# Zero fill moved from chunk 1 into chunk 0 with its own place, and attention steps at other places of chunks 1 to 4

## The chip, the cores and the metric

One core of a Trainium2 chip runs the program alone. The metric is the device time of one execution in microseconds, given as the median of three runs. A profile shows one more execution, engine by engine: TensorE (PE, with its weight loads as PEld), VectorE (DVE), ScalarE (ACT), GpSimd (POOL) and the queue of SyncE (SP), which issues nearly all DMAs.

## What is computed

Three stages follow each other. Their inputs are float32, except `w_in` and `w_out`, which come as 64-bit floats.

```python
B, H, S, D = 4, 8, 576, 64                       # attention, two masks
scores = scale * q @ k.T                         # heads 0-3: the last 32 keys; heads 4-7: every 32nd key
x = softmax(masked scores) @ v                   # reshaped to 2304 tokens x 512
h = x @ w_in                                     # 512 -> 2048
x = (h * clip(h + 3, 0, 6) / 6) @ w_out          # 2048 -> 512
logits = x @ w_gate                              # 8 experts, the best one is taken
e = argmax(logits); g = softmax(logits)[e]; o = sigmoid(x @ w_output_gate)[e]
out = g * o * (relu(x @ w1[e]) @ w2[e])          # 512 -> 1024 -> 512
```

## The kernel before, in words

The 2304 tokens go through the dense layer in six chunks of 384 (c = 0 to 5). In each chunk a loop runs over 16 blocks f of 128 hidden units. `m1(c, f)` does 12 matmuls into a PSUM tile `h`; ACT and DVE make `r` of it (L534, L535) and then the two halves of `gh` (L540, L545); `m2(c, f - 1)`, nine matmuls of 512 columns, adds the block before into three accumulators. Each value is split in two float32r parts, so products take three matmuls.

Attention is cut into 32 groups. Group n passes through three steps: scores (L401, tiles `sa`, `sb`), then the softmax on DVE, ACT and POOL (L413, L418, L422 to L424), transposes (L451, tiles `ta`, `tb`), and the product with v (L468, tile `o`), which ACT and DVE write into `xh` and `xl`, the input of `m1`. One tick does scores of n, transposes of n - 1 and the product of n - 2. Eight ticks stand ahead of chunk 0, the others inside the chunks 0 to 4; the table `AT` says at which f of a chunk its ticks stand, and a chunk that has no entry spreads them evenly. A chunk can start only when the groups that write its tokens are through.

In chunk 0 the 64-bit weights are also loaded (SP, L182, tiles `rawi`, `rawo`, 512 KB each) and converted, on ACT (L192, L193, L216), DVE (L202 to L218) and POOL (L207, L218).

After each chunk the router picks the expert of each token (tile `rt`, allocated in pool `r_p` with one buffer of tag "rt") and POOL scatters the rows of the tokens into a DRAM table `xs_d` (L664). The table has to be zero at its first rows of each expert. `zero_fill` does this: a DVE instruction makes a tile of 132 zeros on each partition (out of `r`, with a bitwise and with 0), and eight DMAs of 792 KB each on SP's queue copy it to the regions of the eight experts. In the kernel before, the zero tile `z` is allocated in `r_p` under tag "rt" too, so the first router tile `rt0` has to wait until `z` has been read.

A scheduler orders the instructions on each engine at build time, the ticks of chunks 1 to 4 with raised priority; each engine then runs its list in order. SP's queue is in order too: an issue that waits for a buffer holds back those behind it.

`o_s` is a small tile that lives through the whole kernel; its only use is in chunk 5 and later, when the experts are put in order (`o_rest`, `o_over`).

Of the kernel before, what the change touches and what calls it, by code (L numbers as in the profile page):

```python
# [22 lines left out]
def kernel(  # L23
# [71 lines left out]
    acc = const.tile([128, NTILE + 1, E], F16, name="acc")  # L95
    cnt = const.tile([128, 8, E], F32, name="cnt")
    o_m = const.tile([128, 2], F32, name="o_m")
    o_s = const.tile([128, 2, E, E], F32, name="o_s")
    eid = const.tile([128, E], F32, name="eid")
    capc = const.tile([128, E], F32, name="capc")  # L100
    first_i = const.tile([128, 1], I32, name="first_i")
# [41 lines left out]
        nc.sync.dma_start(out=wgo[:, :, 0:E], in_=w_gate.rearrange("(c p) e -> p c e", p=128))  # L143
        nc.sync.dma_start(out=wgo[:, :, E:2 * E], in_=w_ogate.rearrange("(c p) e -> p c e", p=128))

    zf = []

    def zero_fill(es):
        if not zf:

            zf.append(r_p.tile([128, XW // 4], F32, tag="rt", name="z"))
            nc.vector.tensor_scalar(out=zf[0].bitcast(I32), in0=gh_t[1, 0][1][:, 0:XW // 4].bitcast(I32), scalar1=0,
                                    scalar2=None, op0=ALU.bitwise_and)
        z = zf[0]
        r = CAPS[0] // 128
        for e in es:
            nc.sync.dma_start(
                out=xs_d[e * NT:e * NT + r * 128, :].rearrange("(p r) (a c) -> p (r a) c", p=128, a=4),
                in_=z.unsqueeze(1).to_broadcast([128, r * 4, XW // 4]),
            )  # L160

# [533 lines left out]
    def o_rest():  # L697

        V = nc.vector
        ps = counts(NTILE, "cnt")  # L700
        V.tensor_copy(cnt[:, 0, :], ps)

        V.scalar_tensor_tensor(out=cnt[:, 2, :], in0=cnt[:, 0, :], scalar=float(E), in1=prio, op0=ALU.mult,
                               op1=ALU.add)
        V.scalar_tensor_tensor(out=cnt[:, 2, :], in0=cnt[:, 1, :], scalar=65536.0, in1=cnt[:, 2, :], op0=ALU.mult,
                               op1=ALU.add)
        sh = [128, E, E]
        key = cnt[:, 2, :]
        V.tensor_tensor(out=o_s[:, 0], in0=key.unsqueeze(1).to_broadcast(sh), in1=key.unsqueeze(2).to_broadcast(sh),
                        op=ALU.is_gt)  # L710
        V.tensor_reduce(out=cnt[:, 3, :], in_=o_s[:, 0], axis=AX.X, op=ALU.add)

        V.tensor_tensor(out=o_s[:, 0], in0=cnt[:, 3, :].unsqueeze(1).to_broadcast(sh),
                        in1=eid.unsqueeze(2).to_broadcast(sh), op=ALU.is_equal)
        V.tensor_tensor(out=o_s[:, 1], in0=o_s[:, 0], in1=eid.unsqueeze(1).to_broadcast(sh), op=ALU.mult)
        V.tensor_reduce(out=cnt[:, 4, :], in_=o_s[:, 1], axis=AX.X, op=ALU.add)
        V.tensor_copy(order_i, cnt[:, 4, :])

    def o_over():

        V = nc.vector
        sh = [128, E, E]
        V.tensor_tensor(out=o_s[:, 1].rearrange("p a e -> p e a"), in0=o_s[:, 0].rearrange("p a e -> p e a"),
                        in1=capc.unsqueeze(1).to_broadcast(sh), op=ALU.mult)
        V.tensor_reduce(out=cnt[:, 5, :], in_=o_s[:, 1].rearrange("p a e -> p e a"), axis=AX.X, op=ALU.add)

        V.tensor_scalar(out=cnt[:, 6, :], in0=cnt[:, 7, :], scalar1=float(RA), scalar2=None, op0=ALU.is_lt)
        V.tensor_tensor(out=cnt[:, 6, :], in0=cnt[:, 6, :], in1=cnt[:, 1, :], op=ALU.mult)
        V.tensor_tensor(out=cnt[:, 7, :], in0=cnt[:, 7, :], in1=cnt[:, 5, :], op=ALU.subtract)
        V.tensor_tensor(out=cnt[:, 7, :], in0=cnt[:, 7, :], in1=cnt[:, 6, :], op=ALU.mult)  # L730
        V.tensor_tensor(out=cnt[:, 5, :], in0=cnt[:, 5, :], in1=cnt[:, 7, :], op=ALU.add)
        V.tensor_tensor(out=cnt[:, 6, :], in0=cnt[:, 0, :], in1=cnt[:, 5, :], op=ALU.subtract)
# [222 lines left out]
    def convert():  # L955
# [3 lines left out]
        for stage, i in ((cv_3, n - 2), (cv_2, n - 1), (cv_1, n)):  # L959
            if 0 <= i < len(wq):  # L960
# [9 lines left out]
             2: [(t, N2, NG) for t in range(3, 10)],  # L970
             3: [(t, N2, NG) for t in range(10, 16)],
             4: [(t, N2, NG) for t in range(16, NG - N2 + 2)]}
    AT = {0: [0, 1, 2, 4, 5, 7, 9, 12]}
    for t in range(T0):
        with tc.high_priority(offset=0):
            at_tick(t, 0, 2 * GPB, alt=True)
# [11 lines left out]
    for c in range(NCH):  # L988
        steps = STEPS.get(c, [])
        at_f = AT.get(c, [i * KF // len(steps) for i in range(len(steps))])  # L990

        def step(f, parts):
            for f2, a in zip(at_f, steps):
                sub = "".join(x for x in (a[4] if len(a) > 3 else "pts") if x in parts)
                if f2 == f and sub:
                    with tc.high_priority(offset=150 if c else 0):
                        at_tick(*a[:3], False, sub)

        for f in range(KF):
            if c == 0:  # L1000
                loads(wl[1] + 4)
                for _ in range(CONVERTS[f]):
                    convert()
            m1(c, f)
            if f:
                for fn in todo[:1]:
                    fn()
                todo = todo[1:]
            step(f, "pt")
            if c == 1 and f < E // 2:  # L1010
                zero_fill([2 * f, 2 * f + 1])
# [242 lines left out]
```

## Time and profile before

| | |
|---|---|
| median of three runs | 879.62 us (879.28 to 881.7) |
| the profiled execution, its own time | 878.62 us |
| its span, first to last instruction | 876.8 us |
| PE / PEld / DVE / ACT / POOL busy | 93 / 83 / 55 / 46 / 19 % |

The span is what the views of the trace cover; the execution's own time is 1.8 us longer, and lies 1.0 us under the median. Runs of this kernel differ by some tenths of a per cent. Busy shares are averages over stages with different limits.

### The profile page before, as it was taken

The page shows a single profiled execution, that of the slowest core. Times are in us where ns is not written, and L with a number is a line of the kernel's source. Part 1 is how long each engine was busy: PE and PEld are TensorE (multiplying, and loading weights), DVE is VectorE, ACT ScalarE, POOL GpSimd, SP SyncE. Part 2 cuts the span into 40 slices and gives each one's busy share as a digit, 9 for nine tenths or more (in the row PEclk, how much of TensorE's full clock was granted, in tenths as well). Part 3 has the DMA queues.
Part 4 walks back from the last instruction along what each step waited for, and adds up shares of the span by engine and source line. Part 5 has one row for each costly group of instructions (what it writes and reads, how often), then busy time and mean ns, then how long its engine had stood idle before and what let it go on. Part 6 is the DMA issues. An engine that isn't in the chain of part 4 may idle for free. (4 is left out here: it accounts for less than half of the span.)

```text
span 876.8 us, 14855 instructions
## 1 busy us (share of the span) xinstructions
PE 815.7 (93%) x5040; PEld 726.2 (83%) x5041; DVE 485.4 (55%) x1394; ACT 405.3 (46%) x1055; POOL 166.0 (19%) x232
## 2 busy tenths in 40 slices
PE   6879888799499999989998999999999999999996
PEld 4668667678488888778887899998899999999995
DVE  4578998852253535534354332335656746766771
ACT  4577766743133533444344422324434545555551
POOL 3355554430021101111021010010011011011110
PEclk9558888999699999979997999999999999999999
DMA  4876222209922211322133000015158556566640
GB/s 132 247 215 184 78 77 93 82 28 201 163 70 41 38 22 28 89 49 46 28 73 74 1 21 18 1 62 158 48 147 235 168 168 185 170 183 210 199 133 20
DMA packets 179191, 91.71 MB, mean 105 GB/s; under 512 B 101369, under 2 KB 165113, under 8 KB 179112
## 3 DMA queue, kind: packets, MB, share of 16 engines
q1 hardware_dynamic: 175992, 81.15, 36.7%
q0 software_dynamic: 3120, 9.59, 2.9%
q8 instruction: 40, 0.66, 0.3%
q14 instruction: 39, 0.32, 0.1%
HBM read 74.63 MB, written 16.60 MB: 104 GB/s over the span
## 5 line engine op out<-in xcount | busy, mean ns | idle before, releaser
L530 PE MATMUL h<-xh,wi 128*128 128x384 f32 x768 | 228.7, 358 | 9.4 <-ACT xh L479 3.4
L554 PE MATMUL x<-wo,gh 128*128 128x512 f32 x864 | 230.6, 402 | 6.7 <-DVE gh L545 4.6
L554 PEld LDWEIGHTS x<-wo,gh 128*128 128x128 f32 x864 | 159.7, 190 | 37.4 <-DVE gh L545 7.0
L530 PEld LDWEIGHTS h<-xh,wi 128*128 128x128 f32 x768 | 148.2, 199 | 19.0 <-ACT xh L479 4.0
L530 PE MATMUL h<-xl,wi 128*128 128x384 f32 x384 | 136.7, 356 | 2.0 <-DVE xl L480 2.0
L535 DVE SCALAR_TENSOR_TENSOR r<-r,h 128x384 f32<-128x384 f32 x96 | 52.8, 550 | 117.1 <-ACT r L534 115.8
L424 POOL TENSOR_TENSOR p<-p,st 126x126 f32<-126x126 f32 (+4 forms) x80 | 56.6, 723 | 244.3 <-DVE st L423 151.9
L534 ACT ACTIVATE r<-h,three 128x384 f32<-128x384 f32 x96 | 55.5, 578 | 94.9 <-PE h L530 67.0
L418 ACT ACTIVATE p<-p,st 96x128 f32<-96x128 f32 (+2 forms) x176 | 67.2, 386 | 57.4 <-DVE st L413 57.3
L545 DVE TENSOR_TENSOR gh<-r,gh 128x384 fp32r<-128x384 f32 x96 | 60.0, 625 | 43.7 <-ACT gh L540 41.9
L540 ACT ACTIVATE gh<-r 128x384 fp32r<-128x384 f32 x96 | 50.3, 524 | 68.9 <-DVE r L535 63.5
L530 PEld LDWEIGHTS h<-xl,wi 128*128 128x128 f32 x384 | 76.6, 200 | 6.6 <-DVE xl L480 2.8
L851 ACT ACTIVATE hh<-eh 128x128 fp32r<-128x128 f32 (+7 forms) x64 | 26.3, 411 | 102.2 <-PE eh L844 94.9
L852 DVE SCALAR_TENSOR_TENSOR hh<-eh,hh 128x128 fp32r<-128x128 f32 (+7 forms) x64 | 29.3, 458 | 74.6 <-ACT hh L851 67.3
L891 POOL DMA_INDIRECT out_dram<-yo,e_i x21 | 21.3, 1015 | 190.9 <-ACT yo L927 186.8
L664 POOL DMA_INDIRECT xs_d<-x2r,idx x18 | 18.8, 1047 | 185.0 <-DVE idx L635 137.6
L401 PE MATMUL sb<-kT,qT 64*96 64x128 f32 (+2 forms) x176 | 35.9, 333 | 4.6 <-DVE st L413 2.2
L401 PEld LDWEIGHTS sb<-kT,qT 64*96 64x96 f32 (+2 forms) x176 | 25.6, 199 | 13.3 <-issue 5.5
L418 ACT ACTIVATION_READ_ACCUMULATOR p<-p,st 96x1 f32 (+2 forms) x176 | 33.5, 190 | 0.0
L468 PE MATMUL o<-pt,v 128*64 128x96 f32 (+2 forms) x352 | 31.1, 301 | 1.3 <-ACT pt L453 1.1
L401 PE MATMUL sa<-kT,qT 64*96 64x128 f32 (+2 forms) x176 | 32.2, 325 | 0.0
L451 PE MATMUL tb<-ident,p 96*128 96x96 f32 (+2 forms) x88 | 17.1, 300 | 15.2 <-DVE rt L599 11.8
(259 smaller groups left out, 1565.9 us busy)
## 6 DMA issues: line engine op xcount, KB each, us to landing
rawi<-in_moe_w_in_dram SPq DMA_DIRECT2D x16, 512.0 KB
rawo<-in_moe_w_out_dram SPq DMA_DIRECT2D x16, 512.0 KB
xs_d<-z SPq DMA_DIRECT2D x8, 792.0 KB
xs<-xs_d SPq DMA_DIRECT2D x28, 128.0 KB
qr<-in_q_dram SPq DMA_DIRECT2D x48, 72.0 KB
kr<-in_k_dram SPq DMA_DIRECT2D x48, 72.0 KB
v<-in_v_dram SPq DMA_DIRECT2D x20, 160.0 KB
er0i<-in_moe_w_dram SPq DMA_DIRECT2D x8, 256.0 KB
```

What stands on the lines that cost most here:

```text
L401: nc.tensor.matmul(s[h2][0:qn, j, 0:kn], lhsT=qt[p0:p0 + 64, q0:q0 + qn], rhs=kt[p0:p0 + 64, k0:k0 + kn], start=True, stop=True)
L418: nc.scalar.activation(out=p[h2][0:qn, j, 0:kn], in_=p[h2][0:qn, j, 0:kn], func=ACTF.Exp, bias=st[0:qn, h2, 0, j:j + 1], scale=-1.0, accum ...
L424: nc.gpsimd.tensor_tensor(out=p[h2][0:qn, j:j + c, 0:kn], in0=p[h2][0:qn, j:j + c, 0:kn], in1=st2.unsqueeze(2).to_broadcast([qn, c, kn]), ...
L468: nc.tensor.matmul(o[64 * h2:64 * h2 + 64, q0 - q00:q0 - q00 + qn], lhsT=vt[0:kn, i, :], rhs=pt[h2][0:kn, j, 0:qn], start=True, stop=True)
L530: nc.tensor.matmul(h, lhsT=w[:, a, kt, :], rhs=x[:, kt, c0:c0 + CH], start=(n == 0), stop=(n == 3 * KD - 1))
L534: nc.scalar.activation(out=r, in_=h, func=ACTF.Relu, bias=three, scale=1.0)
L535: nc.vector.scalar_tensor_tensor(out=r, in0=r, scalar=6.0, in1=h, op0=ALU.min, op1=ALU.mult)
L540: nc.scalar.activation(out=gh[:, 0, :], in_=r, func=ACTF.Copy)
L545: nc.vector.tensor_tensor(out=gh[:, 1, :], in0=r, in1=gh[:, 0, :].bitcast(F32), op=ALU.subtract)
L554: nc.tensor.matmul(acc_ps[c][t], lhsT=gh[:, g, t * 128:(t + 1) * 128], rhs=w[:, a, :], start=(f == 0 and n == 0), stop=(f == KF - 1 and n ...
L851: nc.scalar.activation(out=t[:, 0, 0:C], in_=h[:, 0:C], func=ACTF.Relu)
L852: nc.vector.scalar_tensor_tensor(out=t[:, 1, 0:C], in0=h[:, 0:C], scalar=0.0, in1=t[:, 0, 0:C].bitcast(F32), op0=ALU.max, op1=ALU.subtract)
```

## The change

The zeros no longer lie in a tile of their own under tag "rt" but in `o_s`, which grows from 128 to 132 floats. `zero_fill` is called at the last eight f of chunk 0, once for each expert, instead of twice an f at the first four f of chunk 1. The first call writes all 132 zeros; each later one writes one column again, out of that f's `r`, so that the DMA behind it stands at that f. That write comes after the DMA before has read the tile. The table `AT` gets entries for chunks 1 to 4. `o_rest` and `o_over` use `o_s` through a view and compute the same.

```diff
-    o_s = const.tile([128, 2, E, E], F32, name="o_s")
+    o_s = const.tile([128, XW // 4], F32, name="o_s")
...
-    zf = []
-
-    def zero_fill(es):
-        if not zf:
-
-            zf.append(r_p.tile([128, XW // 4], F32, tag="rt", name="z"))
-            nc.vector.tensor_scalar(out=zf[0].bitcast(I32), in0=gh_t[1, 0][1][:, 0:XW // 4].bitcast(I32), scalar1=0,
-                                    scalar2=None, op0=ALU.bitwise_and)
-        z = zf[0]
+    def zero_fill(e, f):
+
+        z = o_s[:, 0:XW // 4]
+        n = XW // 4 if e == 0 else 1
+        nc.vector.tensor_scalar(out=z[:, 0:n].bitcast(I32), in0=gh_t[0, f][1][:, 0:n].bitcast(I32), scalar1=0,
+                                scalar2=None, op0=ALU.bitwise_and)
         r = CAPS[0] // 128
-        for e in es:
-            nc.sync.dma_start(
-                out=xs_d[e * NT:e * NT + r * 128, :].rearrange("(p r) (a c) -> p (r a) c", p=128, a=4),
-                in_=z.unsqueeze(1).to_broadcast([128, r * 4, XW // 4]),
-            )
+        nc.sync.dma_start(
+            out=xs_d[e * NT:e * NT + r * 128, :].rearrange("(p r) (a c) -> p (r a) c", p=128, a=4),
+            in_=z.unsqueeze(1).to_broadcast([128, r * 4, XW // 4]),
+        )
...
-    AT = {0: [0, 1, 2, 4, 5, 7, 9, 12]}
+    AT = {0: [0, 1, 2, 4, 5, 7, 9, 12], 1: [0, 2, 4, 7, 10, 13], 2: [0, 1, 3, 5, 7, 8, 10], 3: [0, 2, 4, 6, 8, 10],
+          4: [1, 4]}
...
-            if c == 1 and f < E // 2:
-                zero_fill([2 * f, 2 * f + 1])
+            if c == 0 and f >= KF - E:
+                zero_fill(f - KF + E, f)
```

Without an entry the ticks of chunk 1 stood at f 0, 2, 5, 8, 10, 13, those of chunk 2 at 0, 2, 4, 6, 9, 11, 13, those of chunk 3 at 0, 2, 5, 8, 10, 13 and those of chunk 4 at 0 and 8.

The first place is DVE's list in chunk 1, at the first router tile `rt0` (`lg0_0` holds the logits of the first 128 tokens); in brackets stands what each instruction waits for, DMAHW0 to DMAHW7 being the landings of SP's DMAs. Before:

```order
L545 TENSOR_TENSOR gh1_3_2439<-r1_3_2436,gh1_3_2439 128x384 [waits PE_49,Activation_49]
L535 SCALAR_TENSOR_TENSOR r1_4_2479<-r1_4_2479,h1_4_2466 128x384 [waits Activation_49]
L545 TENSOR_TENSOR gh1_4_2482<-r1_4_2479,gh1_4_2482 128x384 [waits PE_49,Activation_49]
L599 COPY rt0_2371<-lg0_0_2375 128x2x8 [waits DMAHW4_49,DMAHW3_49,DMAHW5_49,DMAHW2_49,DMAHW6_49,DMAHW1_49,DMAHW7_49,DMAHW0_49,PE_49]
L535 SCALAR_TENSOR_TENSOR r1_5_2513<-r1_5_2513,h1_5_2500 128x384 [waits Activation_49]
L345 STREAM_TRANSPOSE qT8_2299<-qr8_1788 128x576 [waits DMAHW2_49,DMAHW3_49,DMAHW1_49,DMAHW0_49]
```

And now, where line numbers are four lower:

```order
L341 STREAM_TRANSPOSE qT8_2311<-qr8_1788 128x576 [waits DMAHW2_49,DMAHW3_49,DMAHW1_49,DMAHW0_49]
L418 TENSOR_SCALAR st15_2288<-st15_2288 96x3 [waits Activation_49]
L541 TENSOR_TENSOR gh1_2_2379<-r1_2_2376,gh1_2_2379 128x384 [waits Activation_49]
L419 RECIPROCAL st15_2288<-st15_2288 96x3 [waits DVE_49]
L341 STREAM_TRANSPOSE kT8_2313<-kr8_1793 128x576 [waits DMAHW6_49,DMAHW7_49,DMAHW5_49,DMAHW4_49]
L531 SCALAR_TENSOR_TENSOR r1_3_2444<-r1_3_2444,h1_3_2431 128x384 [waits Activation_49]
L541 TENSOR_TENSOR gh1_3_2447<-r1_3_2444,gh1_3_2447 128x384 [waits PE_49,Activation_49]
L595 COPY rt0_2381<-lg0_0_2385 128x2x8 [waits PE_49]
```

The copy into `rt0` waited for all eight DMAs of the zero fill and for PE; now it waits for PE alone. The transposes of `qr8` and `kr8`, loads that stand behind the zero fill on SP's queue, have moved ahead by about three f.

The second place is SP's queue at the end of chunk 0 (weights, parts of v, the zero fill `xs_d`, then `qr8`). Before:

```order
L182 DMA rawi14_1842<-in_moe_w_in_dram 128x4x256 [waits DMAHW4_49,Activation_49,Pool_49]
L182 DMA rawo14_1962<-in_moe_w_out_dram 128x1024 [waits PE_49]
L182 DMA rawi15_1964<-in_moe_w_in_dram 128x4x256 [waits DMAHW6_49,Activation_49,Pool_49]
L182 DMA rawo15_2014<-in_moe_w_out_dram 128x1024 [waits DMAHW3_49,PE_49]
L289 DMA v4_0_3_1948<-in_v_dram 128x3x64 [waits PE_49,Activation_49]
...
L157 DMA xs_d_93<-z_2237 1536x1x132 [waits DMAHW0_49,DVE_49]
...
L263 DMA qr8_1788<-in_q_dram 32x18x32 [waits DMAHW0_49,PE_49]
```

And now:

```order
L178 DMA rawi14_1844<-in_moe_w_in_dram 128x4x256 [waits DMAHW3_49,DMAHW4_49,Activation_49,Pool_49]
L153 DMA xs_d_93<-o_s_107 1536x1x132 [waits DVE_49]
L178 DMA rawo14_1966<-in_moe_w_out_dram 128x1024 [waits DMAHW5_49,PE_49]
L178 DMA rawi15_1968<-in_moe_w_in_dram 128x4x256 [waits DMAHW6_49,DMAHW7_49,Activation_49,Pool_49]
L153 DMA xs_d_93<-o_s_107 1536x1x132 [waits DVE_49]
L178 DMA rawo15_2020<-in_moe_w_out_dram 128x1024 [waits DMAHW0_49,PE_49]
...
L285 DMA v5_1_3_2309<-in_v_dram 128x3x64 [waits DMAHW6_49,PE_49]
L153 DMA xs_d_93<-o_s_107 1536x1x132 [waits DMAHW7_49,DVE_49]
L259 DMA qr8_1788<-in_q_dram 32x18x32 [waits DMAHW0_49,PE_49]
```

Eight pieces stood in a row behind the last part of v; now they stand one by one between the weight loads `rawi12` to `rawo15` and the parts of v, the last of them still just ahead of `qr8`. Each waits for its own DVE write.

The third place is PE's list at the end of chunk 2, between the product of group 22 (`o22`) and the transposes of group 23 (`ta23`), the last group that writes tokens of chunk 3. Before:

```order
L468 MATMUL o22_3827<-pt22_3710,v24_0_0_3295 64x96
L554 MATMUL x2_2_0_3182<-wo15_2121,gh2_15_4073 128x512 x3
L554 MATMUL x2_2_1_3183<-wo15_2121,gh2_15_4073 128x512 x3
L554 MATMUL x2_2_2_3184<-wo15_2121,gh2_15_4073 128x512 x3
L530 MATMUL h3_0_4085<-xh_116,wi0_548 128x384
...
L530 MATMUL h3_1_4193<-xh_116,wi1_741 128x384
L451 MATMUL ta23_3839<-ident_94,p23_0_3740 128x96 x3
```

And now, where ahead of these rows, but behind `o22`, stand nine matmuls of `m2` and the 12 of `h2_15` too:

```order
L550 MATMUL x2_2_2_3213<-wo14_2072,gh2_14_4051 128x512
L526 MATMUL h3_0_4091<-xh_116,wi0_548 128x384
L550 MATMUL x2_2_0_3211<-wo14_2072,gh2_14_4051 128x512 x2
L550 MATMUL x2_2_1_3212<-wo14_2072,gh2_14_4051 128x512 x2
L550 MATMUL x2_2_2_3213<-wo14_2072,gh2_14_4051 128x512 x2
L526 MATMUL h3_0_4091<-xl_117,wi0_548 128x384
L526 MATMUL h3_0_4091<-xh_116,wi0_548 128x384
L447 MATMUL ta23_3761<-ident_94,p23_0_3690 128x96 x3
```

Between the two steps stood 15 matmuls of `m1` and `m2`; now 33 stand there. At the end of chunk 3, around group 29, PE's list is as before.

## Rows read from the trace of the kernel before

**Rows 1.** The page: busy us of each engine (share of the span) xinstructions.

```profile
PE 815.7 (93%) x5040; PEld 726.2 (83%) x5041; DVE 485.4 (55%) x1394; ACT 405.3 (46%) x1055; POOL 166.0 (19%) x232
```

**Rows 2.** Waits: who <- for whom: us in total, times, longest us.

```profile
DVE rt L599 <- DMA qr<-in_q_dram: 16.5, 1, 16.5
...
PE tb L451 <- DVE rt L599: 11.8, 1, 11.8
```

**Rows 3.** Timeline of DVE, chunk 1: start, duration, instruction [idle before <-releaser].

```profile
213.07 0.56 DVE L545 TENSOR_TENSOR gh<-r,gh 128x384 fp32r<-128x384 f32 x1 [0.59 <-ACT gh L540]
230.11 0.17 DVE L599 COPY rt<-lg 128x16 f32<-128x16 f32 x1 [16.48 <-DMA qr<-in_q_dram]
...
231.86 0.78 DVE L345 STREAM_TRANSPOSE qT<-qr 128x576 f32<-128x576 f32 x1 [1.12 <-DMA qr<-in_q_dram]
```

**Rows 4.** Timeline of PE in the same stretch.

```profile
217.10 1.54 PE L554 MATMUL x<-wo,gh 128*128 128x512 f32 x6
230.43 0.71 PE L451 MATMUL tb<-ident,p 96*128 96x96 f32 x3 [11.79 <-DVE rt L599]
```

**Rows 5.** Timeline of SP's queue: the eight issues of the zero fill.

```profile
194.60 25.55 SPq L157 DMA_DIRECT2D xs_d<-z  x8
```

**Rows 6.** Windows: length, busy us (xinstructions) of PE, PEld, DVE, ACT, POOL, granted clock, DMA share, GB/s.

```profile
70.00:192.00 122.00, 105.58 (x597) 87.00 (x597) 107.48 (x261) 80.81 (x209) 59.52 (x54) 0.89 0.28 85
217.00:231.00 14.00, 2.21 (x12) 1.64 (x11) 0.64 (x2) 0.22 (x1) 0.00 (x0) 0.64 1.18 178
230.43:234.50 4.07, 4.07 (x15) 3.78 (x16) 2.57 (x5) 1.40 (x3) 0.00 (x0) 0.50 0.75 139
...
374.40:384.70 10.30, 8.29 (x43) 7.25 (x42) 2.42 (x17) 4.01 (x16) 2.03 (x3) 0.50 0.45 80
```

**Rows 7.** Timeline of PE from chunk 2 to chunk 3.

```profile
372.26 0.45 PE L530 MATMUL h<-xl,wi 128*128 128x384 f32 x1 [1.41 <-DVE xl L480]
...
374.06 0.47 PE L451 MATMUL ta<-ident,p 96*128 96x96 f32 x3 [0.83 <-POOL p L424]
374.85 0.74 PE L451 MATMUL tb<-ident,p 96*128 96x96 f32 x3 [0.32 <-POOL p L424]
...
380.58 1.01 PE L530 MATMUL h<-xh,wi 128*128 128x384 f32 x2 [1.69 <-ACT xh L479]
```

**Rows 8.** Timeline of DVE in chunk 0: L535 of f 8, 11, 12, 14, 15.

```profile
126.53 0.56 DVE L535 SCALAR_TENSOR_TENSOR r<-r,h 128x384 f32<-128x384 f32 x1 [0.48 <-ACT r L534]
...
149.97 0.56 DVE L535 SCALAR_TENSOR_TENSOR r<-r,h 128x384 f32<-128x384 f32 x1 [1.62 <-ACT r L534]
...
159.27 0.55 DVE L535 SCALAR_TENSOR_TENSOR r<-r,h 128x384 f32<-128x384 f32 x1 [1.52 <-ACT r L534]
...
179.28 0.52 DVE L535 SCALAR_TENSOR_TENSOR r<-r,h 128x384 f32<-128x384 f32 x1
...
185.28 0.56 DVE L535 SCALAR_TENSOR_TENSOR r<-r,h 128x384 f32<-128x384 f32 x1 [3.31 <-ACT r L534]
```

**Rows 9.** Small DVE instructions: groups of chunk 0 (busy us, mean ns), then two of the timeline.

```profile
L422 DVE TENSOR_SCALAR st<-st 96x3 f32<-96x3 f32 x5 | 4.0, 791 | 0.0
...
L422 DVE TENSOR_SCALAR st<-st 126x1 f32<-126x1 f32 x4 | 0.6, 140 | 0.0
...
175.80 3.35 DVE L422 TENSOR_SCALAR st<-st 96x3 f32<-96x3 f32 x1
...
194.35 0.23 DVE L152 TENSOR_SCALAR z<-r 128x132 int32<-128x132 int32 x1
```

**Rows 10.** Timeline of SP and of ACT in chunk 0: two weight loads, and their first readers.

```profile
154.41 0.34 SPq L182 DMA_DIRECT2D rawo<-in_moe_w_out_dram  x1
...
163.21 0.34 SPq L182 DMA_DIRECT2D rawo<-in_moe_w_out_dram  x1
...
158.10 0.67 ACT L193 ACTIVATE rawo<-rawo 128x512 int32<-128x512 uint32 x1 [0.91 <-DMA rawo<-in_moe_w_out_dram]
...
166.90 0.68 ACT L193 ACTIVATE rawo<-rawo 128x512 int32<-128x512 uint32 x1 [3.14 <-DMA rawo<-in_moe_w_out_dram]
```

More of the change, by code (lines that the diff above doesn't have):

```diff
@@ L699, in o_rest @@
         V = nc.vector
+        sel = o_s[:, 0:2 * E * E].rearrange("p (a b e) -> p a b e", a=2, b=E)
         ps = counts(NTILE, "cnt")
@@ L708, in o_rest @@
         key = cnt[:, 2, :]
-        V.tensor_tensor(out=o_s[:, 0], in0=key.unsqueeze(1).to_broadcast(sh), in1=key.unsqueeze(2).to_broadcast(sh),
+        V.tensor_tensor(out=sel[:, 0], in0=key.unsqueeze(1).to_broadcast(sh), in1=key.unsqueeze(2).to_broadcast(sh),
                         op=ALU.is_gt)
-        V.tensor_reduce(out=cnt[:, 3, :], in_=o_s[:, 0], axis=AX.X, op=ALU.add)
-        V.tensor_tensor(out=o_s[:, 0], in0=cnt[:, 3, :].unsqueeze(1).to_broadcast(sh),
+        V.tensor_reduce(out=cnt[:, 3, :], in_=sel[:, 0], axis=AX.X, op=ALU.add)
+        V.tensor_tensor(out=sel[:, 0], in0=cnt[:, 3, :].unsqueeze(1).to_broadcast(sh),
                         in1=eid.unsqueeze(2).to_broadcast(sh), op=ALU.is_equal)
-        V.tensor_tensor(out=o_s[:, 1], in0=o_s[:, 0], in1=eid.unsqueeze(1).to_broadcast(sh), op=ALU.mult)
-        V.tensor_reduce(out=cnt[:, 4, :], in_=o_s[:, 1], axis=AX.X, op=ALU.add)
+        V.tensor_tensor(out=sel[:, 1], in0=sel[:, 0], in1=eid.unsqueeze(1).to_broadcast(sh), op=ALU.mult)
+        V.tensor_reduce(out=cnt[:, 4, :], in_=sel[:, 1], axis=AX.X, op=ALU.add)
         V.tensor_copy(order_i, cnt[:, 4, :])
@@ L721, in o_over @@
         V = nc.vector
+        sel = o_s[:, 0:2 * E * E].rearrange("p (a b e) -> p a b e", a=2, b=E)
         sh = [128, E, E]
-        V.tensor_tensor(out=o_s[:, 1].rearrange("p a e -> p e a"), in0=o_s[:, 0].rearrange("p a e -> p e a"),
+        V.tensor_tensor(out=sel[:, 1].rearrange("p a e -> p e a"), in0=sel[:, 0].rearrange("p a e -> p e a"),
                         in1=capc.unsqueeze(1).to_broadcast(sh), op=ALU.mult)
-        V.tensor_reduce(out=cnt[:, 5, :], in_=o_s[:, 1].rearrange("p a e -> p e a"), axis=AX.X, op=ALU.add)
+        V.tensor_reduce(out=cnt[:, 5, :], in_=sel[:, 1].rearrange("p a e -> p e a"), axis=AX.X, op=ALU.add)
         V.tensor_scalar(out=cnt[:, 6, :], in0=cnt[:, 7, :], scalar1=float(RA), scalar2=None, op0=ALU.is_lt)
```

## Prediction, made before the changed kernel was run

> **What bounds the kernel now.** The page's busy times come first: PE is busy for 815.7 us of the span of 876.8 [rows 1], so the time goes down by what PE idles or runs at a low clock. The list of waits then says where PE idles. One wait stands out: PE stands 11.8 us, once, for the DVE copy into `rt`, and that copy had itself waited 16.5 us for a DMA [rows 2]. The timelines show the place. DVE ends a `gh` at 213.07 + 0.56 us and starts nothing until 230.11 [rows 3]; PE uses up the work that it has and stands from 218.64 to 230.43 [rows 4].
>
> The view names a load of `qr` as the releaser. That name is not to be trusted here, because the copy waits for nine semaphores and the view takes the one that came last. In DVE's list before, the copy needs the landings of all eight DMAs of the zero fill, since its tile `rt0` takes the buffer of the zero tile `z`. SP issues them from 194.60 us on [rows 5], and the copy starts 35.5 us later, so a piece takes 35.5 / 8 = 4.4 us. In that stretch the DMA engines show a share of 1.18 at 178 GB/s [rows 6]: the zero fill itself is what takes so long.
>
> Two other stages matter. Chunk 0 has DVE busy for 107.5 of 122 us and PE for 105.6 [rows 6]; there a longer list on DVE costs. From chunk 2 to chunk 3 PE waits four times for the last attention group, and its clock is at the lower level (granted clock 0.50) from 374.4 to 384.7 us [rows 6, 7].
>
> **The change part by part.** I make the sum against the profiled execution's 878.62 us and add at the end the 1.0 us by which the median lies above it.
>
> *The shared buffer goes.* In the new list the copy into `rt0` waits for PE alone. The wait of 11.79 us on PE [rows 4] goes. After it PE ran 4.07 us at a granted clock of 0.50, 1.2 of 2.4 GHz [rows 6]; it had stood idle before. Half of that, 2.0 us, comes back. The wait was no head start for later work, since DVE stood in it too [rows 3]. What would be late next is the transpose of `qr8`, which now stands three f earlier and waits for a load behind the last zero piece. Its issue waits for PE's scores of group 15, as before; it is ahead of its use in PE's list by several f. I take 0; the bound is one piece, 4.4 us. Together: **-13.8 us**.
>
> *The attention steps.* At the end of chunk 3 PE's list is unchanged, so there nothing is gained; chunks 1 and 4 show no wait of this kind, so I take 0. From chunk 2 to 3, 33 matmuls instead of 15 now cover the softmax of group 23. The 18 more take at the pace of rows 4 (1.54 us for six) up to 4.6 us, more than the three waits of 1.41, 0.83 and 0.32 us [rows 7]; these 2.6 us go. The fourth wait, 1.69 us from the product of group 23 to `xh`, stays: the same rows of `h3_0` follow it. At the low clock PE was busy 8.29 us [rows 6], so up to 4.1 us come back if the clock stays up, and none if the wait that remains still makes it fall. With three of four waits gone I take 3.0. Together: **-5.6 us**, bounds -2.6 and -6.7 for the two parts.
>
> *The writes.* DVE gets eight instructions in chunk 0. The first has 132 columns and 0.23 us, as the one that goes from chunk 1 [rows 9]; seven have one column. The nearest rows are the one-column instructions of L422 with 0.14 us and those of three columns with a mean of 0.79 us, since some stand while POOL works [rows 9]. That gives 1.2 to 5.8 us; nearer to the lower, at 0.25 us each, it is 2.0 us. DVE is 88% busy there, so I count all of it.
>
> *The writes' waits.* Each write but the first waits until the piece before has landed, and behind it on DVE stand `gh`, the conversions and the softmax, for which PE waits. A piece takes 4.4 us. The f of chunk 0 follow each other in (185.28 - 126.53) / 7 = 8.4 us on average, the last two in 6.0 [rows 8]. So each piece has landed, with 1.6 us to spare at the tightest: 0. The bound is a piece behind two weight loads of 512 KB, which at 178 GB/s take 2.9 us each: 10.2 us, 1.8 us over the mean pitch, seven times, 12.6 us.
>
> *The weight loads.* They now follow zero pieces on SP's queue. ACT already waits for two of them, 0.91 and 3.14 us [rows 10], so here a delay is not hidden. The pieces go out just after the `r` of f 11 and f 12, at 149.97 and 159.27 us; the loads behind them went out at 154.41 and 163.21 [rows 8, 10], 4.4 and 3.9 us later, as long as a piece takes. So little meets: 0.8 us, between 0 and 8.8 for two whole pieces. Together with the writes: **+2.8 us**. What DVE and PE gain or lose by the new order at the end of chunk 0 I can't price from rows; I take 0, within 2 us either way.
>
> *The view of `o_s`* changes nothing that runs: the same instructions at the same sizes, long after the last piece.
>
> Sum: 878.6 - 13.8 - 5.6 + 2.8 = 862.0; as a median **863**.
>
> The Trainium skill has a rule that speaks against the writes. Its page "SBUF — State Buffer", section "Who interferes with whom", says that a tensor_scalar on VectorE can take a second port that it shares with GpSimd, and that the one which comes second then stands until the other is through. The trace agrees that this form stretches: one L422 took 3.35 us at 175.80 [rows 9]. By the rule every write could stand behind a POOL instruction, which is the third rival below; the sum would then be 871 instead of 863.
>
> **The rivals.** *Only the stall goes (14%).* The wait that stays from chunk 2 to 3 keeps the clock low, or chunk 0 costs twice what I think: 863 + 3 to 863 + 5.6, about 868. For it: four waits there became one, not none.
>
> *More comes back (10%).* The writes cost only 1.2 us, no load is late, the clock stays up, and the new order at the end of chunk 0 fills a wait there: 863 - 1.6 - 1.1 - 2, about 858. Against it: DVE is the fullest engine in chunk 0.
>
> *POOL holds the writes (7%).* With 0.79 us each the writes take 5.8 us, and POOL, busy 59.5 of 122 us [rows 6], is held as often: 863 + 3.8 + 3.8, about 871. The longest row, 3.35 us for every write, would take 23 us and eat the whole gain. For it: the mean of the five instructions of 96x3 is more than five times that of the four of 126x1, for little more data. Against it: those four, in the same chunk, took 0.14 us each.
>
> *Slower (3%).* The zero pieces hold DVE in chunk 0. The price per write is what a piece takes beyond the pitch of 8.4 us, seven times. The gain of 16.6 us is eaten when it is 2.4 us, so when a piece lands 10.8 us after its write instead of 4.4. Two weight loads ahead of each piece make 10.2. With late conversions on top it would be 883. Against it: the DMA share in chunk 0 is 0.28 [rows 6], so queues are mostly empty.
>
> *No change (2%).* Something else holds DVE at the same place until 230 us, such as the load of `qr8`, and chunk 0 pays for the writes: about 879. Against it: the list of what the copy waits for has PE alone.
>
> **How the numbers follow.** My forecast has 64%, by itself 858 to 868. The range of 855 to 872 adds the second and third cases and most of the fourth, and leaves out the last two and the tails of the others, less than 2 in 10. A measurement of this kernel tells 0.3%, some 2.6 us, from no change. Faster by more than that: 0.95; within: 0.02; slower: 0.03.
>
> **What would show it.** Right: in chunk 1 no DVE wait for a DMA over 3 us, and no PE wait over 2 us; PE dense from chunk 1 to the end of chunk 2, one wait near 1.7 us at `xh` before chunk 3 and a shorter low-clock spell there; the stretch from chunk 3 to chunk 4 unchanged; the eight issues of `xs_d` spread over chunk 0, 6 to 9 us apart. Chunk 0 itself would last some 3 us longer. Wrong: DVE waits for landings at the one-column writes, such writes of over 0.8 us, ACT waits for `rawo` of more than 4 us, or a new DVE wait at the transpose of `qr8`.

## The result, and the profile after

The changed kernel takes 866.43 us (median of 4 runs, 866.08 to 867.82); the kernel before, run beside it on the same chip, takes 879.45 (878.48 to 881.70). The ratio is 0.9851, interval 0.9829 to 0.9873: faster by 1.5%. The profiled execution took 866.75 us, its span is 865.1.

The page's busy times of the changed kernel:

```profile
PE 812.8 (94%) x5040; PEld 721.4 (83%) x5041; DVE 488.5 (56%) x1401; ACT 406.8 (47%) x1055; POOL 165.3 (19%) x232
```

PE's busy time is 2.9 us less than in [rows 1] while the span is 11.7 us shorter: mostly idle time went. Windows of the changed kernel: chunk 0 and the stretch of the old stall at the times of [rows 6], then the passage from chunk 2 to chunk 3; columns as there.

```profile
70.00:192.00 122.00, 100.94 (x555) 81.84 (x554) 108.25 (x252) 78.80 (x195) 59.31 (x51) 0.88 0.56 139
...
217.00:231.00 14.00, 14.00 (x91) 12.49 (x91) 2.94 (x7) 4.96 (x10) 0.00 (x0) 1.00 0.23 52
...
366.00:376.00 10.00, 8.58 (x64) 7.50 (x63) 5.25 (x22) 5.68 (x19) 1.64 (x2) 1.00 0.44 76
```

From 217 to 231 us PE is now busy throughout at the full clock, where it had 2.21 us of work before. From chunk 2 to chunk 3 the clock stays up. In chunk 0, though, PE does 555 matmuls in the 122 us in which it did 597: that stretch has become slower (in part because chunk 0 begins 2.1 us later in this execution).

DVE's timeline in chunk 1, the place of [rows 3]:

```profile
207.63 0.54 DVE L531 SCALAR_TENSOR_TENSOR r<-r,h 128x384 f32<-128x384 f32 x1
...
210.01 0.78 DVE L341 STREAM_TRANSPOSE qT<-qr 128x576 f32<-128x576 f32 x1 [1.18 <-DMA qr<-in_q_dram]
...
212.20 0.78 DVE L341 STREAM_TRANSPOSE kT<-kr 128x576 f32<-128x576 f32 x1 [0.82 <-DMA kr<-in_k_dram]
...
217.68 0.17 DVE L595 COPY rt<-lg 128x16 f32<-128x16 f32 x1 [1.63 <-PE lg L594]
```

The wait of 16.48 us is gone; the copy into `rt` waits for PE's logits, and the two transposes wait about a microsecond each for their loads.

PE's timeline from chunk 2 to chunk 3, the place of [rows 7]:

```profile
368.30 0.72 PE L464 MATMUL o<-pt,v 128*64 128x96 f32 x12
370.44 0.62 PE L526 MATMUL h<-xh,wi 128*128 128x384 f32 x2 [1.42 <-ACT xh L475]
```

Of the four waits only the last is left, with 1.42 us in place of 1.69.

The writes of the zeros in chunk 0 in DVE's timeline, with two of the issues behind them in SP's:

```profile
130.57 0.22 DVE L150 TENSOR_SCALAR o_s<-r 128x132 int32<-128x132 int32 x1
...
130.81 0.68 SPq L153 DMA_DIRECT2D xs_d<-o_s  x1
...
138.61 0.15 DVE L150 TENSOR_SCALAR o_s<-r 128x1 int32<-128x1 int32 x1 [1.08 <-DMA xs_d<-o_s]
...
146.51 0.55 SPq L153 DMA_DIRECT2D xs_d<-o_s  x1
...
153.61 0.15 DVE L150 TENSOR_SCALAR o_s<-r 128x1 int32<-128x1 int32 x1 [0.28 <-DMA xs_d<-o_s]
...
195.23 0.14 DVE L150 TENSOR_SCALAR o_s<-r 128x1 int32<-128x1 int32 x1
```

The eight take 1.3 us, and two of them wait 1.4 us together for the piece before to land. Those pieces were issued at 130.81 and 146.51 us, so their landings set the next write free 7.8 and 7.1 us after the issue.

To place gains and losses, I read the start of DVE's first `r` in each chunk from the timelines and take differences. The table has them for all runs of the study (microseconds, profiled execution), with the median and the ratio to the kernel before on the same chip.

| kernel | chunk 0 | chunk 1 | chunk 2 | chunk 3 | median | ratio (interval) |
|---|---|---|---|---|---|---|
| before | 123.8 | 94.2 | 97.5 | 94.3 | 879.45 | |
| changed | 129.3 | 80.4 | 91.5 | 94.3 | 866.43 | 0.9851 (0.9829 to 0.9873) |
| 1 own place alone | 126.2 | 93.0 | 99.2 | 94.2 | 881.65 | 1.0009 (0.999 to 1.0027) |
| 2 steps alone | 123.8 | 91.7 | 94.0 | 93.1 | 873.31 | 0.9927 (0.9909 to 0.9946) |
| 3 zero fill alone | 128.6 | 80.4 | 92.7 | 93.8 | 866.22 | 0.9831 (0.9813 to 0.985) |
| 4 no piece at f 11 | 129.1 | 80.4 | 91.3 | 94.3 | 867.37 | 0.9851 (0.9833 to 0.987) |
| 5 chunk 1, ACT's queue, own place | 126.0 | 98.0 | 98.0 | 94.3 | 888.89 | 1.01 (1.0083 to 1.0118) |
| 6 chunk 1, ACT's queue, shared | 126.0 | 96.6 | 99.5 | 94.4 | 887.6 | 1.0075 (1.0054 to 1.0097) |
| 7 changed, ACT's queue | 123.0 | 79.9 | 91.2 | 93.8 | 858.78 | 0.9758 (0.9742 to 0.9775) |
| 8 before, with writes | 119.7 | 94.3 | 96.8 | 95.0 | 876.75 | 0.9954 (0.9941 to 0.9967) |
| 9 changed, shared buffer | 124.9 | 80.4 | 91.5 | 94.5 | 863.67 | 0.9826 (0.9802 to 0.9851) |
| 10 one by one in chunk 1 | 122.0 | 107.6 | 87.8 | 94.1 | 883.54 | 1.0047 (1.0032 to 1.0063) |
| 11 changed, one write | 134.1 | 83.3 | 89.2 | 93.0 | 870.16 | 0.9882 (0.9858 to 0.9906) |
| 12 as 7, other steps in chunk 3 | 122.7 | 79.9 | 91.2 | 90.7 | 855.95 | 0.9731 (0.9706 to 0.9755) |

Ahead of chunk 0 the same work took 70.0 us in the profile of before and 72.1 in that of the changed kernel; over all runs it is 70.0 to 73.4. That part of a difference does not come from the edits.

### The profile page after: what moved, and what is told of

Read it like the earlier page. It is cut to its first block, busy times and chain, and to the rows that moved or that the text cites. A ratio compares the mean times of both kernels' runs of the same rounds, so it can differ in the third digit from the quotient of the medians.

```text
span 865.1 us, 14861 instructions
## 1 busy us (share of the span) xinstructions
PE 812.8 (94%) x5040; PEld 721.4 (83%) x5041; DVE 488.5 (56%) x1401; ACT 406.8 (47%) x1055; POOL 165.3 (19%) x232
## 5 line engine op out<-in xcount | busy, mean ns | idle before, releaser
L526 PEld LDWEIGHTS h<-xh,wi 128*128 128x128 f32 x768 | 146.2, 197 | 17.1 <-ACT xh L475 3.6
L397 PE MATMUL sa<-kT,qT 64*96 64x128 f32 (+2 forms) x176 | 31.6, 320 | 0.0
L203 POOL TENSOR_TENSOR cvi<-cvi,rawi 128x512 int32<-128x512 int32 x16 | 24.1, 1504 | 37.2 <-DVE cvi L201 21.9
```

Of the source, the lines that this page charges most:

```text
L397: nc.tensor.matmul(s[h2][0:qn, j, 0:kn], lhsT=qt[p0:p0 + 64, q0:q0 + qn], rhs=kt[p0:p0 + 64, k0:k0 + kn], start=True, stop=True)
L526: nc.tensor.matmul(h, lhsT=w[:, a, kt, :], rhs=x[:, kt, c0:c0 + CH], start=(n == 0), stop=(n == 3 * KD - 1))
```

## The experiments

### 1 to 3: the parts of the change by themselves

Run 1 is the kernel before with the zeros in a place of their own:

```diff
-            zf.append(r_p.tile([128, XW // 4], F32, tag="rt", name="z"))
+            zf.append(const.tile([128, XW // 4], F32, name="z"))
```

> The kernel before, with the zeros in a place of their own; the eight pieces still go out in chunk 1, and the attention steps stay. Theory: the stall came from the buffer that the zeros shared with rt0. Then the 11.8 us wait of PE and 2.0 us of low clock behind it go and nothing else changes: 879.5 - 13.8 = 865.7. Rival: the length of the zero fill was the cause whatever buffer it reads, since the load of qr8 stands on SP's queue behind eight pieces; then DVE stands for most of 10 us at the transpose of qr8, and the time is 872 to 879.

It gained nothing: 881.65 us, ratio 1.0009. The rival was right in its mechanism, and the time even lies above its 872 to 879. DVE's timeline of run 1 in chunk 1:

```profile
213.50 0.17 DVE L599 COPY rt<-lg 128x16 f32<-128x16 f32 x1 [2.50 <-PE lg L598]
...
219.52 0.56 DVE L535 SCALAR_TENSOR_TENSOR r<-r,h 128x384 f32<-128x384 f32 x1 [2.67 <-ACT r L534]
235.01 0.78 DVE L345 STREAM_TRANSPOSE qT<-qr 128x576 f32<-128x576 f32 x1 [14.93 <-DMA qr<-in_q_dram]
```

SP's queue in the same run:

```profile
197.82 25.75 SPq L157 DMA_DIRECT2D xs_d<-z  x8
223.67 9.30 SPq L263 DMA_DIRECT2D qr<-in_q_dram  x4
```

The copy into `rt0` now waits for PE alone and runs at 213.50 us. But the transpose of `qr8` stands behind it in DVE's list and waits 14.93 us, since SP is through with the eight issues only at 223.6 us and `qr8` lands some 11 us later. PE then stands 10.46 us. There were two holds, one behind the other, and the first covered the second.

Run 2 is the kernel before with the new `AT` table alone, run 3 the changed kernel with the old one.

> The kernel before with the new attention steps alone. Theory: three of the four waits from chunk 2 to chunk 3 and the low clock there go, 5.6 us as predicted or up to 7 us as the changed kernel's trace reads: 872.5 to 873.9, with the stall of 11.8 us in chunk 1 still there. Rival: the attention steps bring nothing by themselves, and the re-ordering from chunk 2 to chunk 3 came with the zero fill: 877 to 880.

> The changed kernel with the attention steps of before. Theory: the stall's 13.8 us go and chunk 0 pays 3.5 us or so (5.7 us in the changed kernel's trace, of which some 2 us stood in the start-up): 868.5 to 870, if the waits from chunk 2 to chunk 3 are those of before. Rival: moving the zero fill alone already puts more matmuls ahead of the transposes of group 23, and brings most of what the steps were credited with: 865 to 867.

Run 2 measured 873.31 us, a gain of 0.7%, as expected. Run 3 measured 866.22, as fast as the whole change: its rival was right. The two gains, 7.3 and 14.4 us between the medians, don't add: the whole change gains 13.0. PE's timeline of run 3 from chunk 2 to chunk 3:

```profile
370.58 0.62 PE L526 MATMUL h<-xh,wi 128*128 128x384 f32 x2 [1.05 <-ACT xh L475]
```

With the steps of before, three of the four waits of [rows 7] are gone here too, and the granted clock from 366 to 376 us is 1.00, the upper level. Moving the zero fill made the scheduler put the work at the end of chunk 2 in another order; what I had credited to the steps came with it. The steps alone do it too: in run 2 one such wait is left, 1.06 us, and the clock there is 1.00. Either edit is enough for these waits, and the steps add nothing to the moved zero fill that can be told from the noise. In the table, chunk 2 is 4.8 us shorter than before in run 3 and 6.0 in the changed kernel; the other chunks take those 1.2 us back.

### 4: where chunk 0 pays

In the changed kernel one weight load is late. SP, ACT, DVE and PE in its timeline, in order of time:

```profile
153.79 0.55 SPq L153 DMA_DIRECT2D xs_d<-o_s  x1
154.92 0.35 SPq L178 DMA_DIRECT2D rawo<-in_moe_w_out_dram  x1
...
162.35 0.67 ACT L189 ACTIVATE rawo<-rawo 128x512 int32<-128x512 uint32 x1 [3.44 <-DMA rawo<-in_moe_w_out_dram]
...
163.52 0.55 DVE L531 SCALAR_TENSOR_TENSOR r<-r,h 128x384 f32<-128x384 f32 x1 [1.89 <-ACT r L530]
...
165.55 1.65 PE L550 MATMUL x<-wo,gh 128*128 128x512 f32 x3 [2.41 <-ACT gh L536]
```

`rawo14` goes out right behind a piece and its first reader starts 7.4 us after its issue; before, 3.7 us (154.41 to 158.10, [rows 10]). ACT's next work, DVE's `r` and PE stand behind it. Run 4 has no piece at f 11:

```diff
-            if c == 0 and f >= KF - E:
-                zero_fill(f - KF + E, f)
+            if c == 0 and 7 <= f and f != 11:
+                zero_fill(f - 7 - (f > 11), f)
```

> The changed kernel with the pieces at f 7 to 10 and 12 to 15 of chunk 0, so that none goes out just ahead of the load rawo14. Theory: in the changed kernel rawo14 landed 7.4 us after its issue because a piece stood ahead of it, and ACT's wait of 3.4 us went on to DVE and PE; without it 3 us come back, 863 to 864. Rival: what chunk 0 lost is the price of eight writes on a nearly full DVE and of the waits for landings, which are the same here: 866 to 867, with another load late in place of rawo14.

It measured 867.37 us, no gain; the rival was nearer. The list of waits of run 4 from 126 to 204 us (total, times, longest) shows what changed and what did not:

```profile
PE x L550 <- ACT gh L536: 4.1, 3, 2.3
...
DVE o_s L150 <- DMA xs_d<-o_s: 2.7, 1, 2.7
ACT rawo L189 <- DMA rawo<-in_moe_w_out_dram: 2.6, 2, 1.6
```

The same stretch of the changed kernel:

```profile
ACT rawo L189 <- DMA rawo<-in_moe_w_out_dram: 5.0, 3, 3.4
...
PE x L550 <- ACT gh L536: 4.4, 3, 2.4
...
DVE o_s L150 <- DMA xs_d<-o_s: 1.4, 2, 1.1
```

And of the kernel before:

```profile
ACT rawo L193 <- DMA rawo<-in_moe_w_out_dram: 4.0, 2, 3.1
...
PE x L554 <- ACT gh L540: 0.5, 1, 0.5
```

The wait of 3.44 us is gone, a write now waits 2.7 us for a landing, and PE waits for `gh` nearly as long as in the changed kernel. Chunk 0 lasts 129.1 us, as there. One late load was not the cause by itself.

### 5 and 6: the pieces on ACT's queue, in chunk 1

```diff
-            nc.sync.dma_start(
+            nc.scalar.dma_start(
```

Run 5 does this to run 1, run 6 to the kernel before.

> As the first run (zeros in a place of their own, pieces in chunk 1, old attention steps), with the eight pieces issued on ACT's queue, so that the load of qr8 stands behind none on SP's. Theory, formed after the first run: two things held DVE at the same time, rt0's buffer and the place of qr8 behind the pieces on SP's queue. With both gone the stall's 13.8 us go: 864 to 868. Rival: the pieces fill the DMA engines themselves, so that qr8 lands as late from a queue of its own: 873 to 881.

> The kernel before, with the eight pieces issued on ACT's queue; the zeros still share rt0's buffer. Theory of the two holds: the buffer alone is enough to stop DVE until the last piece has landed: no gain, 877 to 882, with DVE waiting some 14 us at the copy into rt0. Rival: the place on SP's queue is the whole cause and the buffer does no harm: 864 to 868.

Both are slower, at 888.89 and 887.6 us, for a reason that none of the four expectations has. ACT's timeline of run 5:

```profile
198.53 0.92 ACTq L157 DMA_DIRECT2D xs_d<-z  x1
...
199.51 10.82 ACTq L157 DMA_DIRECT2D xs_d<-z  x3
210.38 0.52 ACT L540 ACTIVATE gh<-r 128x384 fp32r<-128x384 f32 x1 [10.31 <-issue]
210.40 12.92 ACTq L157 DMA_DIRECT2D xs_d<-z  x3
223.43 0.58 ACT L534 ACTIVATE r<-h,three 128x384 f32<-128x384 f32 x1 [12.53 <-issue]
```

The first two issues take 0.65 and 0.92 us; three more hold ACT for 10.82 us and the last three for 12.92, so ACT does no work for 10.3 and then 12.5 us, and PE stands 6.68 and 8.07 us for `gh`. SP's four issues of `qr8` are spread over 13.34 us in this run although no piece stood on SP's queue. Its list of waits from 200 to 232 us has the reason:

```profile
SPq L263 <- DMA xs_d<-z: 35.3, 7, 10.8
```

The issues of `qr8` and `kr8` themselves wait for landings of the pieces, from whichever queue those come. So another queue did not part the load from the pieces, and the pair can't tell the buffer from the queue: ACT's hold hides both. What it shows is that eight pieces within some 25 us hold whatever issues them.

### 7 and 8: the same pieces on ACT's queue in chunk 0, and the writes without pieces

Run 7 is the changed kernel with the edit of run 5. Run 8 is the kernel before with one-column writes at the last eight f of chunk 0, into `o_s`, which nothing reads there:

```diff
+            if c == 0 and f >= KF - E:
+                nc.vector.tensor_scalar(out=o_s[:, 0, 0, 0:1].bitcast(I32), in0=gh_t[0, f][1][:, 0:1].bitcast(I32),
+                                        scalar1=0, scalar2=None, op0=ALU.bitwise_and)
```

> The changed kernel, with its eight pieces issued on ACT's queue, so that no weight load stands behind one on SP's. Theory: chunk 0 costs 5 us more than before because weight loads land late behind pieces; then 3 to 4 us come back: 862 to 863.5. Rival: the cost is that of the writes, of their waits for landings or of the DMA engines that are shared on any queue: 865.5 to 868, since those stay.

> The kernel before, with one one-column write into the place of the experts' order at each of the last eight f of chunk 0, which nothing reads; the zero fill stays as it was. It prices the writes without the pieces. Theory: the writes cost what they take on DVE, 1.3 us: 880.5 to 882.5. Rival: the new order that they bring on the engines in chunk 0 costs the 5 us that the changed kernel lost there: 884 to 886.

Run 7 measured 858.78 us, ratio 0.9758 (0.9742 to 0.9775), clear of the changed kernel's interval, and more than the theory asked. Chunk 0 falls from 129.3 to 123.0 us. Paced by the writes, each piece is issued in 0.54 to 0.65 us on ACT's queue. Its waits for loads in the second half of chunk 0:

```profile
DVE o_s L150 <- DMA xs_d<-o_s: 2.5, 2, 1.5
ACT rawo L189 <- DMA rawo<-in_moe_w_out_dram: 1.3, 2, 0.8
ACT rawi L189 <- DMA rawi<-in_moe_w_in_dram: 1.3, 1, 1.3
```

The waits for `rawo` are 1.3 us where the changed kernel has 5.0; the waits for landings are longer (2.5 against 1.4). That speaks for the queue rather than for the DMA engines that both queues share, if the order of the instructions is left aside.

Run 8 fell outside both expectations: the eight writes made the kernel faster, 876.75 us, ratio 0.9954 (0.9941 to 0.9967). Each takes 0.14 or 0.15 us. Chunk 0 is 4.1 us shorter than before, with the old stall behind it unchanged (PE stands 11.77 us). The writes do no work that is read, so I put the gain down to the order that the scheduler makes around them: in the traces 105 of PE's first 900 matmuls stand at another place than before, by their tile names without numbers. This limits what run 7 says: counted in the same way, run 7 and the changed kernel differ in 92 places, run 7 and run 8 in 20. In the nearly equal order of runs 7 and 8, the pieces cost chunk 0 3.3 us (123.0 against 119.7). How much of the 6.3 us between the changed kernel and run 7 is the queue and how much the order stays open.

### 9: the place undone

```diff
+    zf = []
...
-        z = o_s[:, 0:XW // 4]
+        if not zf:
+            zf.append(r_p.tile([128, XW // 4], F32, tag="rt", name="z"))
+        z = zf[0]
```

> The changed kernel with its zeros back in the buffer that rt0 takes; pieces and steps stay as changed. It undoes the place alone. Theory, formed after the first runs: the stall is a matter of when the eight pieces are issued, not of the buffer; in chunk 0 the last piece has landed before rt0 wants the buffer, so nothing is lost: 866 to 867.5. Rival: the place is a needed half of the change, and rt0 waits again for a landing: 869 to 878.

It measured 863.67 us (861.53 to 867.22), no slower than the changed kernel and even below the theory's 866 to 867.5; its mechanism holds, and the place was not needed. DVE's timeline of run 9:

```profile
205.31 0.78 DVE L345 STREAM_TRANSPOSE qT<-qr 128x576 f32<-128x576 f32 x1 [1.16 <-DMA qr<-in_q_dram]
...
213.00 0.17 DVE L599 COPY rt<-lg 128x16 f32<-128x16 f32 x1 [1.62 <-PE lg L598]
```

The last piece is issued at 192.13 us, so it is through when `rt0` wants the buffer at 213. All five engines have the same list as in the changed kernel, names apart. So run 9 is also a second look at that order: chunk 0 took 124.9 us here and 129.3 there. Of the 5.5 us that the changed kernel's chunk 0 lost, 4.4 lie within what these two executions of one order differ by. In the windows from 150 to 175 us the granted clock is 0.86 here and was 0.80 there; ACT's longest wait for `rawo` is 2.65 against 3.44 us.

### 10 and 11: one by one in chunk 1, and in a row in chunk 0

Run 10 has the pieces at f 0 to 7 of chunk 1. Those of f 6 and 7 come behind the scatter of chunk 0's tokens, so they put zeros on rows that the reference keeps; the instructions are the same in number and size.

```diff
-        nc.vector.tensor_scalar(out=z[:, 0:n].bitcast(I32), in0=gh_t[0, f][1][:, 0:n].bitcast(I32), scalar1=0,
+        nc.vector.tensor_scalar(out=z[:, 0:n].bitcast(I32), in0=gh_t[1, f][1][:, 0:n].bitcast(I32), scalar1=0,
...
-            if c == 0 and f >= KF - E:
-                zero_fill(f - KF + E, f)
+            if c == 1 and f < E:
+                zero_fill(f, f)
```

> The changed kernel with its pieces one by one at f 0 to 7 of chunk 1 in place of the last eight of chunk 0, still on SP's queue. Theory: what matters is that pieces go out one at a time; then qr8 stands behind two pieces instead of eight, DVE waits some 4 to 8 us for it, and chunk 0 gets its time back: 862 to 870. Rival: chunk 1, with the loads of groups 16 to 18 in it, has no room for 35 us of pieces however they are spread: 874 to 882.

It measured 883.54 us: the rival was nearer. The list of waits from 195 to 290 us:

```profile
DVE o_s L150 <- DMA xs_d<-o_s: 31.6, 7, 7.4
```

All seven one-column writes wait for the piece before, 31.6 us in all; `qr8` itself waits only 0.72 us. An f of chunk 1 lasts about 5 us in the changed kernel where one in the second half of chunk 0 lasted 8.4 [rows 8], and here each write starts 6.2 to 7.2 us after the issue of the piece that it waits for. Chunk 1 becomes 107.6 us long. This is the slower rival of the prediction, in another chunk: the same edit loses where the pitch is shorter than a piece takes.

Run 11 leaves the seven one-column writes out; the zeros are written at f 8 alone, and the eight pieces stand in a row on SP's queue in chunk 0.

```diff
-        nc.vector.tensor_scalar(out=z[:, 0:n].bitcast(I32), in0=gh_t[0, f][1][:, 0:n].bitcast(I32), scalar1=0,
-                                scalar2=None, op0=ALU.bitwise_and)
+        if e == 0:
+            nc.vector.tensor_scalar(out=z[:, 0:n].bitcast(I32), in0=gh_t[0, f][1][:, 0:n].bitcast(I32), scalar1=0,
+                                    scalar2=None, op0=ALU.bitwise_and)
```

> The changed kernel without its seven one-column writes: the zeros are written once, at f 8 of chunk 0, and nothing paces the pieces, so all eight stand in a row on SP's queue between the loads rawi12 and rawo12. Theory: the writes are what spreads the pieces out; in a row their issues hold SP for some 25 us as in the kernel before, rawo12 goes out some 16 us late, and ACT, DVE and PE of chunk 0 wait for it: 874 to 886. Rival: pieces and loads share the engines wherever they stand, there is slack for both, and 1.3 us of writes and 1.4 us of their waits come back: 862 to 866.

It measured 870.16 us, between the two expectations: all four executions, 868.23 to 873.25, are slower than those of the changed kernel, though the intervals of the ratios overlap a little. SP, ACT and PE in its timeline:

```profile
132.18 25.42 SPq L154 DMA_DIRECT2D xs_d<-o_s  x8
157.70 3.97 SPq L179 DMA_DIRECT2D rawo<-in_moe_w_out_dram  x1
...
171.49 0.66 ACT L189 ACTIVATE cvo<-rawo 128x512 f32<-128x512 f32 x1 [14.43 <-DMA rawo<-in_moe_w_out_dram]
...
173.25 0.74 PE L317 MATMUL nk<-ident,kn 72*128 72x72 f32 x4 [14.78 <-DVE qT L328]
```

The mechanism is as expected: the row of issues holds SP for 25.42 us, ACT stands 14.43 us for `rawo12`, PE 14.78. Yet chunk 0 is only 4.8 us longer than the changed kernel's: its f 13 to 15 and the start of chunk 1 then follow 2.4 to 5.8 us apart. Chunk 1 lasts 83.3 us, so the old stall is gone in a row too; what pacing saves is the wait in chunk 0, and the writes seem to earn a little more than they cost.

### 12: a version that beats both

Run 12 is run 7 with one more line of steps changed:

```diff
-    AT = {0: [0, 1, 2, 4, 5, 7, 9, 12], 1: [0, 2, 4, 7, 10, 13], 2: [0, 1, 3, 5, 7, 8, 10], 3: [0, 2, 4, 6, 8, 10],
+    AT = {0: [0, 1, 2, 4, 5, 7, 9, 12], 1: [0, 2, 4, 7, 10, 13], 2: [0, 1, 3, 5, 7, 8, 10], 3: [0, 2, 3, 5, 7, 8],
```

> The changed kernel with its pieces on ACT's queue (858.8 us), and chunk 3's attention steps at f 0, 2, 3, 5, 7, 8 in place of 0, 2, 4, 6, 8, 10, so that more matmuls stand between the scores and the transposes of the last group ahead of chunk 4. Theory: as from chunk 2 to chunk 3, the waits of 0.6 and 0.8 us there and most of 5 us of low clock (10 us at a granted clock of 0.5) go: 853 to 856. Rival: the wait for the last group's product stays and the clock falls all the same: 857 to 858.5.

It measured 855.95 us (852.22 to 859.87), ratio 0.9731 (0.9706 to 0.9755), within the theory's 853 to 856. Chunk 3 is 3.1 us shorter. The window from 452 to 460 us, first in run 7, then in run 12:

```profile
452.00:460.00 8.00, 6.68 (x37) 5.76 (x36) 3.98 (x20) 3.70 (x15) 1.61 (x2) 0.63 0.22 49
```

```profile
452.00:460.00 8.00, 7.36 (x36) 7.16 (x36) 3.31 (x10) 3.75 (x12) 1.60 (x2) 0.79 0.07 15
```

The clock is better, 0.79 against 0.63 (from 440 to 452 us 1.00 against 0.96), but doesn't stay up. The waits did not get less, as the theory had it: PE's waits there are 0.59, 0.84 and 1.31 us in run 7, and 2.65 and 0.64 us in run 12, the first of them for `xh`. Both kernels are beaten clearly, run 7 not: the intervals overlap.

## Why the prediction was right, and which of its steps were not

The time came out at 866.43 us for 863 forecast, inside the range. The steps fared worse than the sum.

**What bounds the kernel.** The stall's size was read rightly: chunk 1 is 13.7 us shorter (94.15 to 80.43), for 13.8 predicted (11.8 of wait and 2.0 of low clock). The distrust of the view's name was right too: in the trace of before the last part of the eighth piece lands at 229.99 us and the copy starts at 230.11, while `qr8` is landed in full only at 231.74. What failed is the step behind it, "The shared buffer goes". It took the hold that was in sight for the cause of the stall. [rows 3] show the transpose of `qr8` waiting until 231.86, so with the buffer free DVE would have stood there instead, behind the same pieces; run 1 freed the buffer without gain, and run 9 gave it back without loss. What took the stall away is that the pieces go out in chunk 0. That the forecast held is luck in this point: the change moves the pieces as well, and freeing the buffer alone would have been forecast at the same 13.8 us and brought none.

**The attention steps.** The passage from chunk 2 to chunk 3 is 6.0 us shorter (chunk 2 in the table) for 5.6 predicted, by the waits that I named and a clock that stays up. But the steps are not needed for it: run 3 has most of it without them (4.8 us), as run 2 has a part without the moved zero fill (3.5 us, with the same waits gone). I had compared PE's lists of before and after, which hold both edits.

**The writes** took 1.3 us for 2.0 predicted, and **their waits** 1.4 for 0. "A piece takes 4.4 us" is the step that failed there: that is the pace of eight pieces in a row, and pieces issued one at a time, among the weight loads, were landed 7.8 and 7.1 us after their issue where a write waited for them. The pitch of chunk 0 just has room for that; where it has not, in chunk 1 in run 10, the waits come to 31.6 us, more than the bound of 12.6 that I gave for chunk 0.

**The weight loads and the order.** "So little meets: 0.8 us" rests on the distances of before, 4.4 and 3.9 us between piece and load; the new list puts `rawo14` 1.1 us behind its piece, and its reader started 3.7 us later after the issue than before. In ACT's waits for `rawo` this came to 5.0 us where before had 4.0, so 1.0 for 0.8: the price was near, the reason was not. (`rawo15` went out at 172.22 us instead of 163.21 [rows 10], but SP waited 7.3 us for PE there and not behind a piece.) Chunk 0 as a whole lost 5.5 us in the profile against 2.8 predicted, and 1.2 us in the second execution of the same order (run 9). As far as the runs show, the mis-sized term is the new order at the end of chunk 0, which I took as 0 within 2 us: a new order is worth 4.1 us of gain in run 8, and PE's waits for `gh` behind ACT went from 0.5 to 4.4 us in the changed kernel, with 4.1 in run 4, where the long wait for `rawo14` is gone, and 4.0 in run 9. Which part of the order makes these waits, and how much of them is the pieces, stays open. Another 2.1 us of the profile's excess lie ahead of chunk 0, where nothing was changed.

**The rivals.** In the profiled execution chunk 0 did cost twice what I thought, a condition of the rival of 868; in run 9 it did not. POOL did not hold the writes: their longest was 0.22 us. The rule of the Trainium skill that I set beside this rival (page "SBUF — State Buffer", section "Who interferes with whom") has the second of two engines on a shared port stand until the other is through. The trace shows no such stand: three of the eight writes, at 130.57, 146.34 and 175.52 us, ran beside a POOL instruction and took 0.22, 0.15 and 0.15 us, no more than the like ones without. The load of `qr8`, taken at 0 with a bound of 4.4 us, made DVE wait 1.18 us.

**The signs.** Of those for right, DVE waits for no DMA over 3 us in chunk 1, PE for nothing over 2 us, and chunk 3 is as long as before; but the issues of `xs_d` stand 6.8 to 12.9 us apart, not 6 to 9. Three of the four for wrong came too, in a small size: waits at the one-column writes, 5.0 us of waits for `rawo` in all (the longest 3.4), and a wait at the transpose of `qr8`.

## What to carry to other kernels

When one wait ends last, ask what the next instruction on that engine would have waited for: two holds on one cause hide each other, and taking away one shows nothing. A long transfer is best issued piece by piece where the pitch of the loop is longer than a piece issued alone takes to land, which here was longer than its pace in a row; compare the two first. A queue that carries no load with a near reader may help further (run 7, where the order may have a share). Where a scheduler orders the work, an edit in one chunk re-orders others, so credit a gain to a part only after that part has run alone.

## What the runs showed of the hardware

Eight pieces of 792 KB in a row keep their issuing engine for some 25 us, on SP as on ACT (25.75 us in run 1, 25.42 in run 11, 25.3 in all in run 5); paced, one issue takes 0.54 to 0.68 us (run 7 and the changed kernel). On ACT, that time is lost for compute (10.31 and 12.53 us in run 5). The pace of a row is 4.4 us a piece (35.5 / 8 in the kernel before); pieces issued one at a time were landed 7.8 and 7.1 us after their issue in the changed kernel, and 6.2 to 7.2 in run 10. The Trainium skill says on the page "DMA: Bandwidth & Descriptors", section "Issuing engines are not separate DMA queues", that issuing from several engines saves only the time that the issue takes, which is usually small beside the DMA itself. In run 5 it is not small, with 10.82 and 12.92 us for three issues each, and run 7 is 7.65 us faster than the changed kernel from another queue, with ACT's waits for `rawo` down from 5.0 to 1.3 us; how much of that is the order stays open.

One order of instructions (the changed kernel and run 9) took between 861.5 and 867.8 us over eight runs on two occasions; of their two profiled executions chunk 0 alone differs by 4.4 us.
